# Early loads in one order with three groups in flight, and list writes at other steps, in an attention and expert-layer kernel

## The chip, the cores and the metric

The kernel runs on one core of a Trainium2 chip. The metric is device time in microseconds (us): three runs of the kernel before gave 456.02, 459.75 and 461.32 us, median 459.75. A core has TensorE (matrix products, written to PSUM), VectorE and ScalarE (elementwise work, both read PSUM), GpSimd (elementwise work on SBUF, and the DMAs whose rows come from an index list) and SyncE, which here only issues DMAs. Each engine works through its own queue in order; semaphores tell one of another. All DMAs run on the core's 16 DMA engines.

## The reference

Attention with a local window and a few global keys, and then a layer of experts in which each token goes to one expert. Shapes: B, H, S, D = 4, 8, 768, 64; 3072 tokens of 512 values, 8 experts, hidden width 1024, all in f32.

```python
scores = q @ k.T / sqrt(D) + bias            # bias: -slope(head) * distance, 96 local keys and 8 global ones
a = exp(scores - max); a = a / (a.sum() + 1e-9)
x = (a @ v)                                  # per token the 8 heads side by side: 3072 x 512
logits = x @ w_gate + modality_bias[modality_id]
e_idx = argmax(logits); gate_w = softmax(logits)[e_idx]
for e in range(8):                           # only the tokens of expert e
    out[mask] = gate_w * (relu(x[mask] @ w1[e]) @ w2[e])
```

## The kernel before

**Attention.** The tokens are 24 blocks of 128 (6 blocks for each of the 4 batches). The program goes in steps 0 to 24. Step n loads q and k of block n+2 and v of block n (`load_q`, `load_k`, `load_v`: one DMA for q, one for k, three for v, all on SyncE's queue), computes the scores of block n (`s_mm`, L228), the exponentials (`red`, L247 on VectorE and L258 on ScalarE), the transposes of block n-1's probabilities (`t_mm`, L272; their copies out of PSUM `t_cp`, L281 and L279) and the product with v of block n-2 (`pv`, L294 and L306; written "P·V" in the prediction), which `xr` scales and SyncE writes to the DRAM tensor `x_rows` (L334). q(n), k(n) and v(n) have three buffers each. Through `gate_a`, `gate_b` and `gate_c` the gate's logits of blocks n-3 and n-4 follow. Queue order of TensorE, VectorE and ScalarE is written out by hand in this part; SyncE's and GpSimd's order is made by the framework's scheduler, which simulates the program.

**What spaces the early loads.** `chained` (L120) counts groups of loads: two halves of q(0)/k(0) are groups 0 and 1, q(1) and k(1) group 2, then q(2)/k(2), v(0), q(3)/k(3), v(1), q(4)/k(4), v(2). A load in group j, with j from 3 to 8, waits until the last load of group j-2 has landed; later loads wait only for their buffers. The small constants (`consts_l`, L1070) are loaded in step 1's part of the program and wait for the latest group then opened, v(1).

**The lists.** When all six blocks of a batch have logits, its routing runs over the following steps (`route_a` to `route_f`; for the first three batches mostly on GpSimd, for the last on VectorE). It gives each token a row in a list sorted by expert, the DRAM tensor `ids_sorted`. `route_c` (L448) writes the list: six indirect DMAs on GpSimd for each batch, each of 128 rows. The first batch's are at steps 13 to 18, one each, the second's at steps 19 to 21, two each; each waits for the P·V product that was last in the program then (`by`, at first `pv_end`). The third's and fourth's are due after step 24, where `rest` takes up what is left over and calls one piece in each second place of the expert part: there the writes of the third batch wait for `last`, the latest activation of ScalarE in the program; those of the fourth for their data alone.

**Experts.** From the first two batches' lists (1536 tokens) `plan_parts` chooses three full tiles of 256 tokens of one expert, e0 to e2, so that the expert part can begin before the last two batches are listed. `ld_x` (L626) reads a tile's rows of the list on SyncE: at step 22, for all three. `gather_x` (L631) fetches the tokens from `x_rows` with two indirect DMAs on GpSimd, 128 rows of 2 KB each: at step 23 for e0 and 24 for e1; each waits for the step's P·V product. The weights of e0 (`rawe0a`, `rawe0b`) are loaded from step 19 on and split into a high and a low part (`split`) by ScalarE and VectorE.

After step 24 TensorE's queue has the transposes of e0 (`x_t`, L679, into PSUM buffers that block 23's probability transposes used just before), then P·V of block 23, the last gates, and the first layer (`l1_unit`, L696 to L698, three products per chunk). A tile then goes through 16 places m: m = 0 to 7 are the first layer, m = 8 to 15 the second (`l2`, L737 to L739). After each place `fill(u, m)` issues what comes next: pieces of `rest`, reads of lists, weights, gathers, splits. When the plan of all tokens is done (it needs the fourth batch's counts), `slist` holds 8 more full tiles s0 to s7 and 2 half ones, and `order` is extended by them; from then on s0's list is read, its weights loaded and its rows gathered. Beside s0 a slot of up to 32 tokens is computed (`few_...`), transposed at L759.

Of the kernel before, what the change touches and what calls it, by code (L numbers as in the profile page):

```python
# [28 lines left out]
NB = S // P  # L29
# [8 lines left out]
U = 256  # L38
NE = 3
NU = 8  # L40
NCHAIN = 9
BE = 2
NS = 8
NGR = 2
# [29 lines left out]
def moe_attention_kernel(  # L74
    ctx, tc, q, k, v, n_global, n_local, w1, q_t, k_t, v_l, v_s, small, w2, out
):
    nc = tc.nc
# [29 lines left out]
    last = [None]  # L107

    def spaced(ins, by=last):

        tc.add_manual_dep(
            ins.ins,
            by[0].ins.name,
            mybir.DependencyInfo(mybir.DependencyClass.Sync, mybir.DependencyReason.DATA),
            reason="spaced",
        )

    groups = []

    def chained(ins, ends=False):  # L120

        j = len(groups)
        if 2 < j < NCHAIN:
            spaced(ins, [groups[j - 2]])
        if j < NCHAIN and ends:
            groups.append(ins)

    def load_q(n):
# [274 lines left out]
    by = [pv_end]  # L403
# [207 lines left out]
    class Slot:  # L611
        straight = True

    fins, nraw = [], [0]

    def mk(name, e_src, o_src, inv_src, xsrc, halves):
        s = Slot()
# [4 lines left out]
    def ld_x(s):  # L622
        n = P * s.halves
        so = nc.sync.value_load(s.o_src, min_val=0, max_val=E * NT)
        s.ui = idp.tile([P, 2, 2], I32, tag="ui", name=f"ui{s.name}")
        nc.sync.dma_start(s.ui[:, 0 : s.halves, :], ids[ds(so, n), 0:2].rearrange("(t p) o -> p t o", p=P))  # L626
# [104 lines left out]
    def l2(s, fc, t):  # L731
        if fc == 0 and not s.po:
            s.po = {t: p_x(f"po{s.name}{t}") for t in range(2)}
        hi, lo = s.hi["b", fc // 2], s.lo["b", fc // 2]
        wv = slice(fc % 2 * 512, fc % 2 * 512 + 512)
        tt = slice(t * P, (t + 1) * P)
        nc.tensor.matmul(s.po[t], s.hh[:, fc, tt], hi[:, wv], start=(fc == 0), stop=False)  # L737
        nc.tensor.matmul(s.po[t], s.hh[:, fc, tt], lo[:, wv], start=False, stop=False)  # L738
        nc.tensor.matmul(s.po[t], s.hl[:, fc, tt], hi[:, wv], start=False, stop=(fc == 7))  # L739

    def few_in(s):
        so = nc.sync.value_load(s.o_src, min_val=0, max_val=E * NT)
# [269 lines left out]
    def at(n, f, *args):  # L1012
        todo.setdefault(n, []).append((f, args))
# [53 lines left out]
    mod = {}  # L1067

    def consts_l():
        spaced(nc.sync.dma_start(cst, small), [groups[-1]])  # L1070
        ints = cst[:, 144:196].bitcast(I32)
        mod["mb"] = cst[:, 128:144].rearrange("p (m e) -> p m e", m=2)
        mod["gi"] = ints[:, 0:4].rearrange("p (j w) -> p j w", j=2)
        mod["mi"] = ints[:, 4:52].rearrange("p (t w) -> p t w", w=2)
# [45 lines left out]
    LAST = NBLK - NB  # L1120
    for b in range(B):
        n0 = b * NB
        eng = nc.gpsimd if b + 1 < B else V
        at(n0 + NB + 3, route_a, b)
        at(n0 + NB + 4, route_e, b)
        at(n0 + NB + 4, route_b, b)
        at(n0 + NB + 5, route_d, b, eng)
        if b + 1 < B:
            at(n0 + NB + 6, route_f, b)
        for j in range(NB):  # L1130
            at(n0 + NB + 7 + (j // 2 if b else j), route_c, b, j)
    at(1, consts_a)
    at(3, consts_b)
    for j in range(8):
# [83 lines left out]
    at(LAST + 1, open_moe)  # L1218
    for c in range(4):
        at(LAST + 1 + c, lambda c=c: ld_w(eslots[0], "a", (c,)))  # L1220
    at(LAST + 4, lambda: [ld_x(s) for s in eslots])
    for u in range(GE):
        at(LAST + 5 + u, lambda u=u: gather_x(eslots[u], True))
    for n, c, h in ((2, 0, 0), (3, 0, 1), (4, 1, 0), (5, 1, 1), (5, 2, None), (6, 3, None)):
        at(LAST + n, split, None, "a", c, False, h)
    at(LAST + 6, lambda: ld_w(eslots[0], "b"))
# [102 lines left out]


    def rest():
        by[0] = last
        late = [job for n in sorted(todo) for job in todo[n]]
        writes = [args for f, args in late if f is route_c]
        g = planned([(f, args) for f, args in late if f is not route_c])
        while True:
            if writes and (writes[0][0], "pi") in rt:
                route_c(*writes.pop(0))
            try:
                next(g)  # L1340
            except StopIteration:
                break
            yield
        assert not writes

    def planned(late):
        for f, args in late:
            f(*args)
            if f is not route_e:
                yield  # L1350
        r = yield from items("b", plan, base[:, B - 1, NB, :], first_used, NI)
        uei, uoi, inv = slots("b", plan, *[t[:, 0:NS] for t in r], NS, 2)
        for u in range(NS):
            slist.append(mk(f"s{u}", uei[0:1, u : u + 1], uoi[0:1, u : u + 1], inv[:, :, u], xd, 2))
        fs.append(few_slot())
        yield
        gr = yield from granules(*r)
        uei, uoi, inv = slots("g", plan, *[t[:, 0:NGR] for t in gr], NGR, 1)
        for u in range(NGR):
            slist.append(mk(f"g{u}", uei[0:1, u : u + 1], uoi[0:1, u : u + 1], inv[:, :, u], xd, 1))  # L1360
        yield
        nl = NGT - NGR
        uei, uoi, inv = slots("l", plan, *[t[:, NGR:NGT] for t in gr], nl, 1)
        V.tensor_copy(lte[:, 0:nl], uei)
        V.tensor_copy(lto[:, 0:nl], uoi)
        V.tensor_copy(ltv[:, 0:nl], inv[:, 0, :])
        yield
# [4 lines left out]
    wrawb = sM.enter_context(tc.tile_pool(name="wrawb", bufs=RB, side="right", reuse_waits="tile"))  # L1372
    man = tc.manual_schedule(engines={ET.Activation})
    man.__enter__()
    bg = rest()
    fs = []

    nslot = NE + NS + NGR
    order = list(eslots)
# [2 lines left out]
    def fill(u, k):  # L1382

        s = order[u]
        nx = order[u + 1] if u + 1 < len(order) else None
        if u < NE and k % 2 == 0:
            next(bg, None)
        if len(order) == NE and len(slist) == NS + NGR:

            order.extend(slist[j] for j in ORDER)  # L1390
        if ahead[1] < min(len(order), u + 4):
            ld_x(order[ahead[1]])
            if ahead[1] == NE:
                few_in(fs[0])
            ahead[1] += 1
        if ahead[0] < min(len(order), u + 3):
            ld_w(order[ahead[0]])
            ahead[0] += 1
        if ahead[2] < min(len(order), u + 3) and ahead[2] < ahead[1]:
            gather_x(order[ahead[2]])  # L1400
            if ahead[2] == NE:
                few_x(fs[0])
            ahead[2] += 1
        if u == 0 and k in (4, 5, 6, 7):
            split(s, "b", k - 4)
        elif k < 8 and k % 2 and ("b", k // 2) in s.raw:
            split(s, "b", k // 2)
        if nx is None:
            return
        if s.halves == 1 and k == 3:  # L1410
            split(nx, "a", 0, early=True)
        if nx.halves == 1 and k in TB:
            split(nx, "b", TB.index(k))
        if s.halves == 1:
            if k in TG:
                split(nx, "a", TG.index(k) + 1)
        elif k >= 8 and k % 2 == 0:
            if ("a", k // 2 - 4) in nx.raw:
                split(nx, "a", k // 2 - 4)
        if s.halves == 2 and k in TX:  # L1420
            x_t(nx, TX.index(k))
# [157 lines left out]
```

## Time and profile before

| | |
|---|---|
| three runs | 456.02, 459.75, 461.32 us; median 459.75 |
| the profiled execution | 457.99 us, of which the span in the profile is 456.3 |
| mean granted TensorE clock | 0.985 |
| TensorE products busy | 437.4 us, 96% of the span |
| VectorE, ScalarE busy | 306.4 us (67%), 273.0 us (60%) |
| GpSimd busy | 117.9 us (26%) |
| DMA | 111.31 MB, mean 244 GB/s |

The profile shows one execution. Its times are counted from the start of the span. A row of a timeline has the start, the length, engine, source line, operation, out<-in by the program's names (numbers left out: `vx<-in_v_l` is the load of any block's v) and, in brackets, how long the engine stood idle just before and what released it. The releaser is inferred: where the engine named had long been done, it was another, often a DMA. SyncE only issues; its rows give the time of issue and not of landing. Busy shares of TensorE are modelled, since its products are pipelined. The granted clock is 1.00 at 2.4 GHz and 0.50 at 1.2 GHz.

### The profile page before, as it was taken

The page shows a single profiled execution, that of the slowest core. Times are in us where ns is not written, and L with a number is a line of the kernel's source. Part 1 is how long each engine was busy: PE and PEld are TensorE (multiplying, and loading weights), DVE is VectorE, ACT ScalarE, POOL GpSimd, SP SyncE. Part 2 cuts the span into 40 slices and gives each one's busy share as a digit, 9 for nine tenths or more (in the row PEclk, how much of TensorE's full clock was granted, in tenths as well). Part 3 has the DMA queues.
Part 4 walks back from the last instruction along what each step waited for, and adds up shares of the span by engine and source line. Part 5 has one row for each costly group of instructions (what it writes and reads, how often), then busy time and mean ns, then how long its engine had stood idle before and what let it go on. Part 6 is the DMA issues. An engine that isn't in the chain of part 4 may idle for free.

```text
span 456.3 us, 12951 instructions
## 1 busy us (share of the span) xinstructions
PE 437.4 (96%) x4856; PEld 382.9 (84%) x4856; DVE 306.4 (67%) x924; ACT 273.0 (60%) x674; POOL 117.9 (26%) x240
## 2 busy tenths in 40 slices
PE   7989999999899799999999999999999999999995
PEld 5778888888777698988889898898988989898993
DVE  7858888888697539688735659657496564647450
ACT  6858878878776336263635548645485554545541
POOL 8130011137726214805032211211312204010101
PEclk9989999999999799999999999999999999999998
DMA  7899999999998727557674767966679766655101
GB/s 249 277 306 328 356 351 362 353 332 328 301 303 283 270 68 246 204 190 268 224 245 146 251 212 256 368 212 226 229 237 368 263 214 237 206 203 186 47 2 52
DMA packets 41671, 111.31 MB, mean 244 GB/s; under 512 B 8815, under 2 KB 10863, under 8 KB 41600
## 3 DMA queue, kind: packets, MB, share of 16 engines
q1 hardware_dynamic: 36640, 97.07, 63.3%
q0 software_dynamic: 4672, 12.85, 7.6%
q8 instruction: 40, 0.66, 0.6%
q10 hardware_dynamic: 288, 0.48, 0.3%
q14 instruction: 31, 0.25, 0.2%
HBM read 96.01 MB, written 14.43 MB: 242 GB/s over the span
## 4 chain that ended last, share of the span: by engine, by line
PE 81%; issue 6%; DVE 4%; DMA 3%; POOL 3%; ACT 2%; SPq 0%; POOLq 0%; DVEq 0%
PE pt L272 7%; PE phs L696 6%; PE phs L698 6%; PE phs L697 6%; PE pos L739 6%; PE pos L738 6%; PE pos L737 6%; PE s L228 6%; PE x L306 5%; PE phe L698 3%; PE x L294 2%; PE phe L696 2%; PE phe L697 2%; PE tx L341 2%; PE poe L737 2%
## 5 line engine op out<-in xcount | busy, mean ns | idle before, releaser
L258 ACT ACTIVATE pr<-sc,nmx 128x168 f32<-128x168 f32 x192 | 81.1, 424 | 21.1 <-DVE nmx L247 21.1
L696 PE MATMUL phs<-xhs,ahs 128*128 128x256 f32 x256 | 72.4, 283 | 0.0
L698 PE MATMUL phs<-xhs,als 128*128 128x256 f32 x256 | 72.3, 283 | 0.0
L697 PE MATMUL phs<-xls,ahs 128*128 128x256 f32 x256 | 72.2, 282 | 0.0
L703 DVE SCALAR_TENSOR_TENSOR hls<-phs,hhs 128x512 fp32r<-128x512 f32 x32 | 22.1, 692 | 55.4 <-ACT hhs L702 55.4
L247 DVE CUSTOM_DVE_ANT_0 sc<-s,tbl 128x168 f32<-128x168 f32 x192 | 51.0, 328 | 8.7 <-PE s L228 7.8
L737 PE MATMUL pos<-bhs,hhs 128*128 128x512 f32 x128 | 51.4, 402 | 0.0
L631 POOL DMA_INDIRECT xgs<-x_rows,uis x16 | 19.9, 1246 | 121.9 <-DMA uis<-ids_sorted 55.7
L739 PE MATMUL pos<-bhs,hls 128*128 128x512 f32 x128 | 50.6, 395 | 0.0
L738 PE MATMUL pos<-bls,hhs 128*128 128x512 f32 x128 | 50.5, 395 | 0.0
L272 PE MATMUL pt<-ident,pr 128*128 128x128 f32 x288 | 45.3, 286 | 4.8 <-ACT pr L258 1.9
L696 PEld LDWEIGHTS phs<-xhs,ahs 128*128 128x128 f32 x256 | 49.0, 191 | 0.5 <-issue 0.2
L697 PEld LDWEIGHTS phs<-xls,ahs 128*128 128x128 f32 x256 | 48.9, 191 | 0.3
L698 PEld LDWEIGHTS phs<-xhs,als 128*128 128x128 f32 x256 | 48.9, 191 | 0.0
L702 ACT ACTIVATE hhs<-phs 128x512 fp32r<-128x512 f32 x32 | 19.1, 597 | 48.5 <-PE phs L698 42.7
L281 DVE COPY pT<-pt 128x384 f32<-128x384 f32 x73 | 38.2, 547 | 13.3 <-PE pt L272 12.6
L272 PEld LDWEIGHTS pt<-ident,pr 128*128 128x128 f32 x288 | 30.2, 141 | 17.1 <-DVE pT L281 5.7
L448 POOL DMA_INDIRECT ids_sorted<-tki,pi x24 | 25.8, 1074 | 49.8 <-issue 16.6
L228 PE MATMUL s<-kt,qt 64*64 64x168 f32 x768 | 36.7, 317 | 1.2 <-DVE nmx L247 1.0
L258 ACT ACTIVATION_READ_ACCUMULATOR pr<-sc,nmx 128x1 f32 x192 | 36.0, 188 | 0.0
L831 POOL DMA_INDIRECT out<-obs,ois x16 | 16.5, 1034 | 72.5 <-ACT obs L830 70.4
L228 PEld LDWEIGHTS s<-kt,qt 64*64 64x64 f32 x768 | 27.3, 136 | 4.7 <-ACT xT L343 1.3
(368 smaller groups left out, 1029.0 us busy)
## 6 DMA issues: line engine op xcount, KB each, us to landing
vx<-in_v_l SPq DMA_DIRECT2D x24, 512.0 KB
kt<-in_k_t SPq DMA_DIRECT2D x23, 464.0 KB
x_rows<-xr SPq DMA_DIRECT2D x24, 256.0 KB
qt<-in_q_t SPq DMA_DIRECT2D x23, 256.0 KB
vl<-in_v_s SPq DMA_DIRECT2D x48, 96.0 KB
rawe0a<-in_moe_w SPq DMA_DIRECT2D x4, 512.0 KB
rawe0b<-in_w SPq DMA_DIRECT2D x4, 512.0 KB
rawe1a<-in_moe_w SPq DMA_DIRECT2D x4, 512.0 KB
```

The lines of the kernel that those rows point to most:

```text
L228: nc.tensor.matmul(ps[h][64 * half : 64 * half + 64, c : c + W], qt[hs, hp, 64 * half : 64 * half + 64], kt[hs, hp, k0 : k0 + W], start=Tr ...
L247: V.tensor_tensor_reduce(out=sc, in0=pss[n, hp // 2][h][:, hp % 2 * W : (hp % 2 + 1) * W], in1=(tbl0 if n % NB == 0 else tbl)[:, hh, :], o ...
L258: last[0] = nc.scalar.activation(pr[:, h * (PRW - W) : h * (PRW - W) + W], sc, AF.Exp, bias=nmx[:, hh : hh + 1], scale=-1.0, accum_out=sum ...
L272: nc.tensor.transpose(tp[:, j * P : (j + 1) * P], pr[:, o : o + P], ident)
L281: V.tensor_copy(pT.rearrange("p a b -> p (a b)"), tp[:, 0 : 3 * P])
L448: ins = nc.gpsimd.indirect_dma_start(out=ids, out_offset=bass.IndirectOffsetOnAxis(ap=pi[:, j : j + 1], axis=0), in_=tki[:, b * NB + j, :] ...
L696: nc.tensor.matmul(o, hi[:, fs], s.xh[:, c, :], start=(c == 0), stop=False)
L697: nc.tensor.matmul(o, hi[:, fs], s.xl[:, c, :], start=False, stop=False)
L698: nc.tensor.matmul(o, lo[:, fs], s.xh[:, c, :], start=False, stop=(c == 3))
L737: nc.tensor.matmul(s.po[t], s.hh[:, fc, tt], hi[:, wv], start=(fc == 0), stop=False)
L738: nc.tensor.matmul(s.po[t], s.hh[:, fc, tt], lo[:, wv], start=False, stop=False)
L739: nc.tensor.matmul(s.po[t], s.hl[:, fc, tt], hi[:, wv], start=False, stop=(fc == 7))
```

## The change

It does four things.

- `chained`: a group of early loads waits for the group three ahead instead of two, and this holds up to group 10 (v(3)) instead of 8. Each load also comes behind the one before it in the queue, in the order in which the program calls them. The constants go through `chained` as well: they stand behind v(1) and ahead of q(4), and wait for v(0).
- The second batch's list writes are at steps 19 and 20, three each. The lists of e0 to e2 are read at step 21, e0's gather is at step 22, e1's at step 23.
- The twelve writes of the third and fourth batch are no longer called by `rest` but by `fill`, one after each place m = 8 to 15: eight beside e0's second layer, four beside e1's. The third batch's wait for `l2_end`, the latest product of the second layer in the program.
- `order` is extended by the remaining tiles only when all list writes have been called.

```diff
-NCHAIN = 9
+NCHAIN = 10
...
-    groups = []
+    groups, queue = [], []
 
     def chained(ins, ends=False):
 
         j = len(groups)
-        if 2 < j < NCHAIN:
-            spaced(ins, [groups[j - 2]])
-        if j < NCHAIN and ends:
+        if j > NCHAIN:
+            return
+        if j > 2:
+            spaced(ins, [groups[j - 3]])
+        if queue:
+            tc.add_manual_dep(
+                ins.ins,
+                queue[-1].ins.name,
+                mybir.DependencyInfo(mybir.DependencyClass.NoSync, mybir.DependencyReason.DATA),
+                reason="in order",
+            )
+        queue.append(ins)
+        if ends:
             groups.append(ins)
...
-        nc.tensor.matmul(s.po[t], s.hl[:, fc, tt], hi[:, wv], start=False, stop=(fc == 7))
+        l2_end[0] = nc.tensor.matmul(s.po[t], s.hl[:, fc, tt], hi[:, wv], start=False, stop=(fc == 7))
...
     def consts_l():
-        spaced(nc.sync.dma_start(cst, small), [groups[-1]])
+        chained(nc.sync.dma_start(cst, small))
...
         for j in range(NB):
-            at(n0 + NB + 7 + (j // 2 if b else j), route_c, b, j)
+            at(n0 + NB + 7 + (j // 3 if b else j), route_c, b, j)
...
-    at(LAST + 4, lambda: [ld_x(s) for s in eslots])
+    at(LAST + 3, lambda: [ld_x(s) for s in eslots])
     for u in range(GE):
-        at(LAST + 5 + u, lambda u=u: gather_x(eslots[u], True))
+        at(LAST + 4 + u, lambda u=u: gather_x(eslots[u], True))
...
     def rest():
-        by[0] = last
+        by[0] = l2_end
         late = [job for n in sorted(todo) for job in todo[n]]
-        writes = [args for f, args in late if f is route_c]
-        g = planned([(f, args) for f, args in late if f is not route_c])
-        while True:
-            if writes and (writes[0][0], "pi") in rt:
-                route_c(*writes.pop(0))
-            try:
-                next(g)
-            except StopIteration:
-                break
-            yield
-        assert not writes
-
-    def planned(late):
+        writes.extend(args for f, args in late if f is route_c)
         for f, args in late:
+            if f is route_c:
+                continue
             f(*args)
             if f is not route_e:
                 yield
...
         if u < NE and k % 2 == 0:
             next(bg, None)
-        if len(order) == NE and len(slist) == NS + NGR:
+        if k >= 8 and writes and (writes[0][0], "pi") in rt:
+            route_c(*writes.pop(0))
+        if len(order) == NE and len(slist) == NS + NGR and not writes:
 
             order.extend(slist[j] for j in ORDER)
```

Lines left out only declare `l2_end`, `writes` and `fs` earlier. LAST is 18, NB 6, NE 3.

## Rows read from the trace of the kernel before

**Rows 1.** The answer by stretches (us, each engine's busy time and count, TensorE's granted clock, DMA share, GB/s).

```profile
...
26.50:29.90 3.40, 3.40 (x68) 2.78 (x67) 0.00 (x0) 0.37 (x2) 1.54 (x8) 0.50 1.02 334
...
152.80:159.60 6.80, 6.33 (x70) 5.32 (x62) 2.94 (x7) 2.03 (x4) 1.78 (x2) 0.50 0.52 180
...
```

**Rows 2.** TensorE's timeline, steps 4 to 6 (start, length; in brackets idle before, releaser).

```profile
...
22.93 1.37 PE L228 MATMUL s<-kt,qt 64*64 64x168 f32 x32
26.10 1.38 PE L294 MATMUL x<-vl,pT 40*64 40x64 f32 x32 [1.79 <-DVE nmx L247]
...
32.17 1.57 PE L228 MATMUL s<-kt,qt 64*64 64x168 f32 x32
...
37.84 1.40 PE L228 MATMUL s<-kt,qt 64*64 64x168 f32 x32
...
```

**Rows 3.** SyncE's timeline (DMA issues), the early loads.

```profile
...
7.05 0.33 SPq L151 DMA_DIRECT2D vx<-in_v_l  x1
...
13.44 0.33 SPq L151 DMA_DIRECT2D vx<-in_v_l  x1
...
16.25 0.35 SPq L131 DMA_DIRECT2D qt<-in_q_t  x1
...
19.03 0.33 SPq L1070 DMA_DIRECT2D cst<-in_small  x1
19.40 0.43 SPq L151 DMA_DIRECT2D vx<-in_v_l  x1
...
```

**Rows 4.** TensorE's timeline, step 22 to the first layer.

```profile
...
132.02 1.15 PE L306 MATMUL x<-vx,pT 128*64 128x64 f32 x32
...
142.69 1.16 PE L294 MATMUL x<-vl,pT 40*64 40x64 f32 x32
...
149.98 0.63 PE L679 MATMUL mte<-ident,xge 128*128 128x128 f32 x4 [1.37 <-issue]
151.78 0.63 PE L679 MATMUL mte<-ident,xge 128*128 128x128 f32 x4 [1.18 <-DMA xge<-x_rows,uie]
152.34 0.82 PE L294 MATMUL x<-vl,pT 40*64 40x64 f32 x32
...
157.99 0.56 PE L696 MATMUL phe<-xhe,ahe 128*128 128x256 f32 x1
...
```

**Rows 5.** GpSimd's timeline, list writes and gathers.

```profile
...
122.34 0.97 POOL L448 DMA_INDIRECT ids_sorted<-tki,pi  x1 [0.30 <-issue]
...
128.67 0.97 POOL L448 DMA_INDIRECT ids_sorted<-tki,pi  x1 [0.30 <-issue]
...
143.48 1.10 POOL L631 DMA_INDIRECT xge<-x_rows,uie  x1 [1.10 <-DMA rawe0b<-in_w]
144.89 0.95 POOL L631 DMA_INDIRECT xge<-x_rows,uie  x1 [0.30 <-issue]
...
```

**Rows 6.** SyncE's timeline, steps 21 and 22.

```profile
...
129.48 0.35 SPq L151 DMA_DIRECT2D vx<-in_v_l  x1
...
135.15 2.15 SPq L626 DMA_DIRECT2D uie<-ids_sorted  x3
...
```

**Rows 7.** Stretches of 10 us, columns as in rows 1.

```profile
...
0.00:10.00 10.00, 7.56 (x96) 6.22 (x96) 6.74 (x46) 6.43 (x25) 8.65 (x49) 1.00 0.75 246
10.00:20.00 10.00, 8.50 (x187) 6.92 (x189) 9.32 (x51) 8.09 (x36) 2.68 (x5) 1.00 0.87 268
...
60.00:70.00 10.00, 9.97 (x235) 8.56 (x234) 8.79 (x51) 7.58 (x33) 2.83 (x15) 1.00 1.04 355
...
```

**Rows 8.** GpSimd's timeline, last list write and few-row gather.

```profile
...
189.75 0.97 POOL L448 DMA_INDIRECT ids_sorted<-tki,pi  x1 [0.30 <-issue]
...
211.02 1.03 POOL L749 DMA_INDIRECT xgf<-x_rows,uif  x1 [0.30 <-issue]
...
```

**Rows 9.** TensorE's timeline, second tile's second layer and few-row transposes.

```profile
...
197.48 0.39 PE L737 MATMUL poe<-bhe,hhe 128*128 128x512 f32 x1
...
221.51 0.43 PE L759 MATMUL mtf<-ident,xgf 32*128 32x32 f32 x4
...
```

More of the change, by code (lines that the diff above doesn't have):

```diff
@@ L612, in moe_attention_kernel @@
         straight = True
-    fins, nraw = [], [0]
+    fins, nraw, l2_end = [], [0], [None]
     def mk(name, e_src, o_src, inv_src, xsrc, halves):
@@ L1374, in moe_attention_kernel @@
     man.__enter__()
+    fs, writes = [], []
     bg = rest()
-    fs = []
     nslot = NE + NS + NGR
```

## The prediction

> **What bounds the kernel now.** I read the busy shares first (the table above): TensorE is at work in 96% of the span. So a change pays only where TensorE stands still or runs slowly. The windows and the granted clock show where: two stretches at 0.50, that is 1.2 instead of 2.4 GHz, 26.50 to 29.90 and 152.80 to 159.60 [rows 1]. Each follows a wait of TensorE, and I looked for the releaser of each in TensorE's timeline.
>
> The first: step 4's scores begin at 22.93; the P·V product of block 2 begins only at 26.10, after 1.79 us of idling, and the next step's scores at 32.17, while the next step takes 32.17 to 37.84 [rows 2]. The row names VectorE's nmx as releaser, but P·V does not read it; it reads v(2). SyncE issued vx(2) at 19.40, right behind the constants at 19.03, which wait for all of v(1); before that q(4) left at 16.25, when k(3) was there, and v(1) at 13.44, when v(0) was there [rows 3]. So v(2) was 6.7 us under way, and late because it was issued late.
>
> The second: TensorE ends the last attention step at 148.6 (149.98 less 1.37), idles 1.37 us, transposes one half of the first expert tile, idles 1.18 us, and gets to the first layer at 157.99 [rows 4]. The transposes read the gathered rows. GpSimd issued that gather at 143.48 and 144.89, though its row list was asked for at 135.15, itself 6.5 us after the last list write at 128.67 [rows 5, 6]; from 144.89 to 151.78 the second half took 6.9 us.
>
> **The change part by part, against the profiled execution** (457.99 us, 1.76 below the median 459.75 of the runs shown).
>
> *Early loads.* Before, a group waits for the one two ahead, constants for v(1); now for the one three ahead, in one order, and the constants stand before q(4). Then v(1) waits for k(2) and q(4), k(4) for v(0), which was there at 13.44; v(2) waits for k(3), there at 16.25 [rows 3], if nothing lands sooner. So v(2) leaves by about 16.3 instead of 19.40, and with 6.7 us it lands by 23.0, before the 24.3 (26.10 less 1.79) at which TensorE asks for it: an estimate with 1.3 us to spare. The DMA engines have room: their share is 0.75 in the first 10 us and 0.87 in the next [rows 7]. Step 4 took 9.24 us against 5.67 for the next [rows 2]: 3.57 us to win, the idle 1.79 and the half clock together. Bounds: 0, if v(2) stays as late; 3.6. I take 3.5. What is late next: k(5), q(5) and v(3), now waiting for groups of v(1) and k(4), needed at 28.4 and 29.8 instead of 32.2 and 33.5; they share the DMA time won. From 60 to 70 us the DMA share is 1.04 beside a full TensorE [rows 7]: little is to be had there, so the lead must come from the idle 2.5 + 1.3 us (0.25 and 0.13 of 10) of the first two windows, 3.8 us, which covers 3.5 barely.
>
> *Writes of the second batch's list in steps 19 and 20, list read in step 21, gathers in steps 22 and 23.* Step 20 issues its second write at 122.34 [rows 5]; the third, now the list's last, follows one write and its pause, 1.3, later: 123.7. With the old 6.5 us to the reads they leave at 130.2, and the three take 2.15 [rows 6]: 132.4. The gather then waits for step 22's P·V, which ends at 133.2 (132.02 plus 1.15, [rows 4]). Its second half leaves 1.4 later, at 134.6, and, with 6.9 us, is there at 141.5, 7 us before 148.6. So both waits go, 1.37 and 1.18, except some 0.4 for the PSUM copies that the transposes follow: P·V of the last block begins at 150.1 instead of 152.34 [rows 4], with no idle behind it that would lower the clock. From there to the first layer 5.65 us passed at 1.2 GHz; at 2.4 GHz I take 3.3, half and a little for waits between engines. The first layer starts at 153.4, 4.6 sooner, and its first 1.6 us at half clock (157.99 to 159.6) shrink by 0.7: 5.3. Bounds: 0 and 1.37 + 1.18 + half of 6.8, 5.95.
> Costs: two writes of 1.0 us each move from step 21 into steps 19 and 20, and one gather pair into step 22, all on GpSimd beside VectorE's copies. No row prices them; bounds −2 and +2 us from their own length, I take 0, since six writes stay six. The second tile's pair comes about where the first's stood. Behind the gather on GpSimd stands the routing of the third batch, up to 2.8 us later; its lists are needed only under the first expert tile. On SyncE the reads now stand before v(22) instead of behind it: see the rivals.
>
> *The last twelve writes.* Third-batch writes now wait for a second-layer product instead of an activation; fourth-batch writes wait for nothing new but are called later, and the remaining tiles are ordered only when none is left, one call later. TensorE waits for none of this: the last write left at 189.75 and the first gather from these lists that TensorE needs at 211.02, for a transpose at 221.51 [rows 8, 9]. With 6.9 us it is there at 217.9, 3.6 us early. Cost 0, covered by that spare; without it see the last rival.
>
> Sum: 457.99 − 3.5 − 5.3 = 449.2; the same off the median is 450.95. I put the prediction between, at **450.0**.
>
> **Rivals.**
> 1. *Only the move of the lists pays* (0.13). v(3) or k(5) is the next late load: the same wait comes one step on. For it: the DMA share above 1 in the loaded stretch. Against it: the idle share before. 457.99 − 5.3 = 452.7, 454.5 off the median.
> 2. *Only the start pays* (0.13). SyncE works in order; held until 130.2 by the list writes, then 2.15 us for the reads, it issues vx(22) not at 129.48 [rows 6] but near 134.0. With 6.7 us it lands at 140.7; TensorE wants it at 142.69 [rows 4], 2.0 later. If the writes land more than 2 us later than I take, TensorE waits in step 24, the clock falls there instead, and the second gain goes: 454.5, 456.3 off the median. The trace speaks a little against it by those 2.0 us.
> The Trainium skill's DMA: Bandwidth & Descriptors, Queues, rings and completion order, says that each DMA engine takes turns, packet by packet, between the queue rows that have work. By that rule the gather from GpSimd's queue would share the engines with v(22). Half a megabyte at the 355 GB/s of the full window [rows 7] is 1.5 us, which would leave 0.5 of the 2.0 us to spare: the sum stays 449.2, and this rival's 454.5 comes nearer. No row here shows the two together.
> 3. *It doesn't do what it says* (0.08): the scheduler leaves GpSimd's gather behind the routing, or SyncE's order as it was, and early loads come no sooner: 458 to 460.
> 4. *Slower* (0.06). With three groups in flight the early loads share the engines evenly instead of following each other, and each lands one group (3 us, 13.44 to 16.25) later. k(1), there at 7.05 when vx(0), which waits for it, leaves [rows 3], would come at about 10. TensorE would wait 3 us in steps 1 to 3, and of its 16 us of work in the first 20 (7.56 + 8.50, [rows 7]) some 7 would run at the lower clock and take twice as long: +10 − 5.3 on 457.99 is 462.7, 464.5 off the median. It decides once k(1) lands later than the bias tables, which GpSimd builds meanwhile, hide. Against it: before, each group was there in the order of issue, 2.8 to 3.4 us apart.
> 5. *Late last lists* (0.05). Emitted later, the fourth batch's last write may also run later: where it is called, behind the fourth product group (1.4 us each) of the second tile's second layer, which begins at 197.48 [rows 9]: 203.1 instead of 189.75. With 6.5 us to the reads, 2.15 for them, some 2 for their landing and 2.8 for the pair ahead, the few-row gather leaves at 216.6 instead of 211.02 and lands 2.0 past its transpose. With a half-clock stretch as after 152 (6.8 us, 3.4 lost) that is 5.4: 454.6. It costs nothing up to 3.6 us of delay.
>
> **Numbers.** The forecast, both gains within 1.5 us, has 0.55: 446.5 to 452.5. Rivals 1 and 2 add 452.7 to 456.3; the range **446 to 457** leaves out 3, 4 and the unknown. About 1% is what runs of this kernel can tell apart: faster means below 455.2. Faster 0.55 + 0.13 + 0.04 of rivals 2 and 5: 0.72. Same: the rest of 2 and 5 (0.14) and 3 (0.06): 0.20. Slower 0.08: rival 4 and a bad end of 3.
>
> **What would show it.** Start: no stretch at half clock near 26 us, step 4 to 5 about 5.6 us, vx(2) issued by 16.5. If vx(2) leaves early and TensorE still waits in step 5, rival 1. Lists: no wait over 0.5 us before the first transposes of the expert tile, no half clock there, gather near 133; if instead P·V of block 22 waits, rival 2. Last lists: a wait at the few-row transpose, rival 5. The step lengths from 30 to 110 us should stay at 5.5. The forecast is wrong if TensorE idles over 2 us anywhere between 20 and 155 us.

## The result, and the profile after

The changed kernel takes 456.08 us (median of 20 runs, 453.12 to 458.86) where the kernel before takes 459.74 (20 runs beside them): ratio 0.9919, 95% interval 0.9894 to 0.9945, so 3.7 us of gain where 8.8 to 9.7 were forecast. The profiled execution took 456.71 us, 1.3 under that of before; its last product starts at 448.83 instead of 450.19.

The page of the changed kernel: busy shares, the clock by slices, the queue of instructions.

```profile
PE 433.4 (95%) x4856; PEld 380.3 (84%) x4856; DVE 306.4 (67%) x924; ACT 273.9 (60%) x674; POOL 120.5 (26%) x240
...
PEclk9999999999999999999999999999999999999998
...
q8 instruction: 40, 0.66, 0.6%
```

The half clock is gone up to TensorE's last product, and still the span is hardly shorter. Line numbers are 10 higher than before. SyncE's issues, TensorE's scores of steps 4 to 6, and stretches, as [rows 3], [rows 2], [rows 1, 7]:

```profile
14.41 0.33 SPq L161 DMA_DIRECT2D vx<-in_v_l  x1
```

```profile
22.55 1.41 PE L238 MATMUL s<-kt,qt 64*64 64x168 f32 x31
...
28.20 1.60 PE L238 MATMUL s<-kt,qt 64*64 64x168 f32 x32
...
33.90 1.39 PE L238 MATMUL s<-kt,qt 64*64 64x168 f32 x32
```

```profile
26.50:29.90 3.40, 3.40 (x68) 2.91 (x70) 2.98 (x11) 2.32 (x9) 0.00 (x0) 1.00 1.03 291
50.00:60.00 10.00, 9.35 (x221) 8.30 (x221) 8.24 (x45) 6.94 (x28) 0.00 (x0) 1.00 1.04 347
60.00:70.00 10.00, 9.49 (x182) 8.13 (x181) 7.93 (x39) 8.30 (x35) 3.62 (x18) 1.00 1.03 338
...
80.00:90.00 10.00, 9.24 (x202) 7.97 (x200) 7.74 (x39) 7.27 (x29) 1.99 (x2) 1.00 1.03 344
...
152.80:159.60 6.80, 5.61 (x71) 4.74 (x66) 3.44 (x8) 2.56 (x5) 1.71 (x2) 1.00 0.80 267
```

vx(2) leaves at 14.41 instead of 19.40 and step 5 begins at 28.20 instead of 32.17: a lead of 3.97 us, and step 4 takes 5.65 us where it took 9.24. Then the lead is lost. P·V's second half (the products with vx) of block 3 starts 3.94 us sooner, of block 8 2.91, of block 11 1.46, of block 14 at 95.93 against 95.89 before. The stretch is full for the DMA engines (share 1.01 to 1.04), and TensorE is busy 9.2 to 9.5 of 10 us. Its timeline shows where it stands:

```profile
51.85 0.39 PE L304 MATMUL x<-vl,pT 40*64 40x64 f32 x10
52.67 0.57 PE L304 MATMUL x<-vl,pT 40*64 40x64 f32 x22 [0.42 <-issue]
...
58.71 0.50 PE L304 MATMUL x<-vl,pT 40*64 40x64 f32 x17 [0.23 <-issue]
...
65.14 0.46 PE L304 MATMUL x<-vl,pT 40*64 40x64 f32 x15 [0.51 <-issue]
...
71.70 0.44 PE L304 MATMUL x<-vl,pT 40*64 40x64 f32 x10 [0.74 <-issue]
...
83.97 0.27 PE L304 MATMUL x<-vl,pT 40*64 40x64 f32 x1 [0.73 <-issue]
...
90.56 1.04 PE L316 MATMUL x<-vx,pT 128*64 128x64 f32 x29 [0.59 <-issue]
```

Read the counts: 22, 17, 15, 10, 1 products of P·V's first half are left behind the stall, then 29 of the second half. The stall walks through the step. Counted from the head of the queue it comes at products 974, 1101, 1227, 1354, 1607 and 1733, that is at steps of 126 or 127 (with as many weight loads, some 253 instructions; the boundary near 1480 passes without a stall), while a step has 122. A late operand would stay at its place. Each stall ends 2.5 to 2.8 us after the start of one of the 40 packets of 16 KB on the instruction queue; at the seven boundaries that follow, none with a stall, the packet had begun 3.0 to 6.8 us before. I call them page stalls, a page being the instructions that one packet brings. Between starts of products the six cost 4.5 us (3.2 as idle time); the expectations below say 3.9, which is the sum without the one at 974.

The transition from the attention to the experts, as [rows 4], [rows 5] and [rows 6]: TensorE, then GpSimd, then SyncE.

```profile
143.66 1.13 PE L304 MATMUL x<-vl,pT 40*64 40x64 f32 x32
...
150.59 1.09 PE L689 MATMUL mte<-ident,xge 128*128 128x128 f32 x8 [0.50 <-ACT pT L289]
151.61 0.69 PE L304 MATMUL x<-vl,pT 40*64 40x64 f32 x32
...
155.52 0.39 PE L369 MATMUL lq<-sel,lps 128*128 128x8 f32 x2 [1.19 <-ACT lps L362]
155.76 0.36 PE L706 MATMUL phe<-xhe,ahe 128*128 128x256 f32 x1
```

```profile
124.36 0.96 POOL L458 DMA_INDIRECT ids_sorted<-tki,pi  x1 [0.30 <-issue]
...
134.41 1.10 POOL L641 DMA_INDIRECT xge<-x_rows,uie  x1 [5.59 <-DMA uie<-ids_sorted]
...
190.04 0.97 POOL L458 DMA_INDIRECT ids_sorted<-tki,pi  x1 [0.30 <-issue]
...
209.66 1.03 POOL L759 DMA_INDIRECT xgf<-x_rows,uif  x1 [0.30 <-issue]
```

```profile
130.72 2.19 SPq L636 DMA_DIRECT2D uie<-ids_sorted  x3
```

The gather leaves at 134.41 instead of 143.48, and of the two waits before the transposes 0.50 us is left, for the copies of block 23's transposes. Block 22's P·V is 0.97 us later than before, e0's first layer 2.2 us sooner. The gain is then lost once more, in e1's first layer: 181.51 to 196.52, 15.0 us against 13.0 before, with stalls for which the profile shows no releaser. The last list writes [rows 8], at 188.35 and 190.04, and the two writes of e0's results behind them in GpSimd's queue, at 191.32 and 192.62, run beside them:

```profile
191.97 0.28 PE L708 MATMUL phe<-xhe,ale 128*128 128x256 f32 x1 [0.59 <-issue]
...
193.42 0.38 PE L706 MATMUL phe<-xhe,ahe 128*128 128x256 f32 x1 [0.82 <-issue]
...
194.86 0.38 PE L708 MATMUL phe<-xhe,ale 128*128 128x256 f32 x1 [0.44 <-issue]
```

### The profile page after: what moved, and what is told of

It reads as the page before. It is cut to its first block, busy times and chain, and to the rows that moved or that the text cites. A ratio compares the mean times of both kernels' runs of the same rounds, so it can differ in the third digit from the quotient of the medians.

```text
span 455.0 us, 12952 instructions
## 1 busy us (share of the span) xinstructions
PE 433.4 (95%) x4856; PEld 380.3 (84%) x4856; DVE 306.4 (67%) x924; ACT 273.9 (60%) x674; POOL 120.5 (26%) x240
## 4 chain that ended last, share of the span: by engine, by line
PE 86%; issue 6%; POOL 3%; DVE 2%; ACT 2%; POOLq 0%; ACTq 0%
PE pt L282 8%; PE phs L706 6%; PE phs L708 6%; PE phs L707 6%; PE s L238 6%; PE pos L749 6%; PE pos L748 6%; PE pos L747 6%; PE x L316 5%; PE x L304 3%; PE phe L706 3%; PE phe L708 3%; PE phe L707 3%; PE poe L747 3%; PE poe L749 2%
## 5 line engine op out<-in xcount | busy, mean ns | idle before, releaser
L641 POOL DMA_INDIRECT xgs<-x_rows,uis x16 | 20.4, 1277 | 121.1 <-PE mts L689 73.7
L712 ACT ACTIVATE hhs<-phs 128x512 fp32r<-128x512 f32 x32 | 19.1, 598 | 48.4 <-PE phs L708 40.6
L458 POOL DMA_INDIRECT ids_sorted<-tki,pi x24 | 28.1, 1170 | 50.1 <-issue 20.4
L841 POOL DMA_INDIRECT out<-obs,ois x16 | 16.6, 1034 | 72.5 <-ACT obs L840 70.4
```

The lines of the kernel that those rows point to most:

```text
L458: ins = nc.gpsimd.indirect_dma_start(out=ids, out_offset=bass.IndirectOffsetOnAxis(ap=pi[:, j : j + 1], axis=0), in_=tki[:, b * NB + j, :] ...
```

## The experiments

Each set ran on one chip, with the kernel before timed beside it; the sets ran on five chips, here named by number; which chip the result above comes from is not on record. The ratios are those on record; the quotient of the medians shown differs from them by up to 0.0044. Theory A: the early lead is lost to TensorE's instructions coming late while the DMA engines are full. Theory B: v comes late. Theory C: the twelve writes' new places cost something.

### Chip 1: the parts alone, and less traffic

*Early loads alone* (the edits of `chained` and `consts_l`, `NCHAIN = 10`, on the kernel before).

> The kernel before with the new order and spacing of the early loads alone; lists, gathers and the last twelve writes stay as before. Theory A (late instruction pages): in the changed kernel the lead of 3.97 us at step 5 is spent between 50 and 96 us in stalls of TensorE of 0.45 to 0.96 us, each at one and the same count of instructions (every 253 or so) and 2.5 to 2.8 us after a 16 KB packet of the instruction queue began, while the DMA engines are full. It will be spent here too: the half clock near 26 us is gone, P.V of block 15 starts within 0.5 us of the kernel before, and the time is 0 to 0.7 us under it (ratio 0.9985 to 1.000). Rival (my forecast's step 1): the lead lasts to the end of the attention and the time is 3.0 to 3.8 us under (ratio 0.992 to 0.9935).

457.55 us, ratio 0.9953 (0.9928 to 0.9978). Between the two: some 2.1 us are gained, theory A's "0 to 0.7" is wrong as the rule, and so is my 3.5. In the profiled execution six page stalls (products 468, 595, 974, 1101, 1227, 1354; 2.9 us together) take the lead back: block 8 is level with before. That one execution says less than twelve timed ones.

*List moves alone.*

```diff
-            at(n0 + NB + 7 + (j // 2 if b else j), route_c, b, j)
+            at(n0 + NB + 7 + (j // 3 if b else j), route_c, b, j)
...
-    at(LAST + 4, lambda: [ld_x(s) for s in eslots])
+    at(LAST + 3, lambda: [ld_x(s) for s in eslots])
...
-        at(LAST + 5 + u, lambda u=u: gather_x(eslots[u], True))
+        at(LAST + 4 + u, lambda u=u: gather_x(eslots[u], True))
```

> The kernel before with the second batch's list writes at steps 19 and 20 and the reads and gathers one step earlier, nothing else. Theory A, by which the early loads bring nothing to the end: all of the changed kernel's gain is from here, the gather of e0 issues near 135 us, the first layer of e0 starts 2 to 4 us before that of the kernel before, and the time is 2.5 to 4 us under it (ratio 0.991 to 0.9945). Rival: the transition's gain is only the early loads' lead in other clothes; the time is within 1 us of before (ratio 0.998 to 1.002).

455.59 us, ratio 0.9934 (0.9909 to 0.9960): 3.0 us. From P·V's second half of block 22 to e0's first layer it takes 10.5 us; with the early loads alone 13.4. The rival is out. The start, whose loads are as before, came 2.3 us sooner than in the first profile of before (block 3), without a half clock near 26 us.

*Smaller zeroing*, on the changed kernel and on the kernel before.

```diff
-        idv = ids.rearrange("(p r) w -> p (r w)", p=P)
-        spaced(nc.sync.dma_start(idv[:, j * nid // 8 : (j + 1) * nid // 8], zrow))
+        r0 = j * NT + (0 if j == 5 else 1280)
+        idv = ids[r0 : r0 + 512].rearrange("(p r) w -> p (r w)", p=P)
+        spaced(nc.sync.dma_start(idv, zrow[:, 0:64]))
```

> The changed kernel, but of the list tensor only the 512 rows of each expert that lie round the end of its list are zeroed beforehand (the rows that are read past the lists' ends are among them): 8 writes of 32 KB instead of 8 of 194 KB, 1.29 MB less between 25 and 75 us, which is 3.7 us of DMA at the 345 GB/s of that stretch. Theory A: the stalls at the page boundaries fall from 3.9 us in sum to under 1.5, P.V of block 15 starts 2 to 3.5 us before that of the changed kernel, and half or more of this reaches the end: 1 to 3 us under the changed kernel (ratio to the kernel before 0.985 to 0.990). Theory B (the new order of loads makes v's data late, since the stalls sit in P.V): order and sizes of the loads are unchanged, so the stalls stay at 0.45 to 0.96 us each and the ratio at 0.992.

> The kernel before with the same smaller zeroing of the list tensor. Theory A: its TensorE comes 4 us later into the full stretch and stalls there for some 0.4 us in all, so there is next to nothing to win: P.V of block 15 within 0.6 us of the kernel before, ratio 0.998 to 1.000. Rival (the zero writes slow the attention in any case, by taking DMA time from the loads): 2 to 3.5 us gained as in the changed kernel, ratio 0.992 to 0.996.

On the changed kernel: 455.04 us, 0.9916 (0.9886 to 0.9945). After block 4 one page stall is left (0.37 us at product 974), before it there are two (0.74 and 0.39 at 468 and 595), with the same loads in the same order. That speaks against theory B, but weakly: on chip 2, below, the changed kernel has none in this stretch with the zeroing as it was. A lead of 2.1 us on the kernel before at block 4 is 2.4 at block 14:

```profile
70.00:80.00 10.00, 10.00 (x239) 8.87 (x231) 8.37 (x48) 8.27 (x37) 0.88 (x1) 1.00 1.00 332
```

But the time is that of the changed kernel. Block 22 is 2.4 us sooner than in the first profile of the changed kernel; 1.0 is left after the gates, since the granted clock is 0.50 from 154.5 to 157.9, and 0.7 at the end. Theory A's 1 to 3 us under the changed kernel did not come. On the kernel before: 457.83, 0.9973 (0.9945 to 1.0001), between the two expectations; not told apart.

### Chip 10: without the twelve, doubled writes, and the kernel before again

*Early loads and list moves, the last twelve writes as before* (both edits above), then *the same with the smaller zeroing*.

> The changed kernel without its last part: early loads and list moves as changed, the last twelve list writes called as in the kernel before. Theory C: the twelve writes' new places cost something. In the changed kernel the first layer of e1 takes 15.0 us with five stalls between 189 and 195 us, behind the fourth batch's writes; in the kernel before and with the lists moved alone it takes 13.0 us with three. Here it is 12.9 to 13.2 us, and the time is 1.2 to 2 us under the changed kernel (ratio to before 0.987 to 0.989). Rival (forecast's step 4: the twelve cost nothing): e1's first layer stays near 15 us, ratio 0.991 to 0.993.

> The same with the smaller zeroing of the list tensor (512 rows for each expert instead of all). If the two losses are separate (page boundary stalls by full DMA engines, e1's first layer by the twelve writes) they add: no stall over 0.3 us in P.V between 45 and 96 us, e1's first layer 13.0 us, ratio 0.984 to 0.988. If the transition at 145 to 160 us hides what the attention wins, it is no better than the kernel without the smaller zeroing (0.987 to 0.989).

448.39 us, 0.9861 (0.9821 to 0.9900), and 447.63, 0.9855 (0.9823 to 0.9887). Better than the changed kernel's 0.9919, but not for the reason expected: on this chip e1's first layer has no stalls in any kernel. From e1's first layer to e2's it is 23.55 us in the kernel before too, where chip 1 had 25.0 to 27.0. So this set does not test theory C, and ratios of different chips can't be set against each other. The smaller zeroing is again worth nothing at the end, and against the expectation it does not clear the page stalls: 0.94 us at product 595 and 0.62 at 1101 come even so.

*Each zero write twice.*

```diff
-        spaced(nc.sync.dma_start(idv[:, j * nid // 8 : (j + 1) * nid // 8], zrow))
+        for _ in range(2):
+            spaced(nc.sync.dma_start(idv[:, j * nid // 8 : (j + 1) * nid // 8], zrow))
```

> The changed kernel with each zero write of the list tensor made twice: 1.55 MB more between 25 and 75 us, 4.5 us of DMA at 345 GB/s. Theory A: the stalls of TensorE at its instruction pages grow from 3.9 us in sum to 6 to 9, P.V of block 15 starts 2 to 5 us later than in the changed kernel, ratio to before 0.996 to 1.004. If the stalls have to do with something else, P.V of block 15 moves by less than 1 us and the ratio stays at 0.992.

475.14 us, 1.0447 (1.0413 to 1.0481), far outside both. SyncE's queue says why:

```profile
46.00 6.77 SPq L1129 DMA_DIRECT2D ids_sorted<-zrow  x2
52.88 0.37 SPq L141 DMA_DIRECT2D qt<-in_q_t  x1
```

The second write goes to the rows of the first and waits until that has landed; the loads of q, k and v stand behind it, for some 6 us in each step. TensorE waits for k (15.5 us in eight waits), at half clock in between. My experiment measured a held queue, not traffic: the DMA share fell to 0.7.

*The kernel before, profiled again.*

> The kernel before, profiled a second time. The forecast took two half clock stretches of the first profile (26.5 to 29.9 and 152.8 to 159.6 us) as part of the kernel. Two other kernels with its early loads unchanged had no such stretch near 26 us and reached P.V of block 3 1.9 and 2.3 us earlier. If the stretches are chance of one execution, here at least one of them is gone or elsewhere, and P.V of block 3 starts 1.5 to 2.5 us before 33.5; if they belong to the kernel, both are there again within 2 us.

```profile
26.50:29.90 3.40, 3.40 (x58) 2.85 (x56) 1.79 (x6) 2.52 (x10) 1.01 (x5) 1.00 1.01 341
136.20:139.50 3.30, 3.30 (x20) 3.27 (x17) 1.97 (x5) 1.69 (x6) 0.00 (x0) 0.50 0.15 34
153.30:160.00 6.70, 5.07 (x79) 4.16 (x80) 2.17 (x5) 2.10 (x3) 1.89 (x2) 0.50 0.83 287
```

No half clock at 26.5, against [rows 1]; a new one at 136; the one at 153 is there. The second half of block 3's P·V starts 1.67 us sooner than in the first profile. And this kernel, with its old loads, falls 4.0 us behind the first profile between blocks 3 and 12, with five page stalls of 4.2 us (products 848, 974, 1101, 1354, 1607). So the stalls are not the change's alone; how many come differs from execution to execution.

### Chip 9: the parts beside each other

> The changed kernel itself, beside three of its parts on one chip, because the ratios measured so far come from different chips. Theory C (the twelve writes' new places cost): 0.4 to 0.6% over the kernel with the early loads and list moves alone. Rival (the chips differ): within 0.2% of it, whatever the level of both.

> Early loads and list moves, the last twelve writes as before. Theory C: 0.986 to 0.988 of the kernel before, and the changed kernel 0.991 to 0.993. Rival: both the same within 0.2%.

> The list moves alone. If the two parts add, this is 0.993 to 0.994 as measured, and 0.4 to 0.6% over the kernel with both parts. If the early loads' lead is spent in the full stretch (theory A), it equals the kernel with both parts within 0.2%.

> The early loads alone. If the parts add: 0.994 to 0.997 of the kernel before. Theory A: 0.9985 to 1.000.

| kernel | us | ratio to before (455.28) |
|---|---|---|
| changed | 449.11 | 0.9835 (0.9800 to 0.9869) |
| loads and lists | 449.75 | 0.9847 (0.9814 to 0.9880) |
| lists alone | 450.86 | 0.9901 (0.9869 to 0.9933) |
| loads alone | 453.59 | 0.9956 (0.9925 to 0.9987) |

The parts add (0.9901 x 0.9956 = 0.9857), and the twelve writes cost nothing here: 23.54 or 23.55 us from e1's first layer to e2's in all four. The whole change is worth 7.5 us on this chip by the ratio, 6.2 by the medians. Its transition with the loads alone, then with the whole change:

```profile
142.47 1.15 PE L316 MATMUL x<-vx,pT 128*64 128x64 f32 x32
...
148.16 0.63 PE L689 MATMUL mte<-ident,xge 128*128 128x128 f32 x4 [1.44 <-ACT ahe L678]
150.32 1.09 PE L689 MATMUL mte<-ident,xge 128*128 128x128 f32 x4 [1.54 <-DMA xge<-x_rows,uie]
...
155.73 0.37 PE L706 MATMUL phe<-xhe,ahe 128*128 128x256 f32 x1
```

```profile
144.37 1.15 PE L316 MATMUL x<-vx,pT 128*64 128x64 f32 x32
...
149.12 1.09 PE L689 MATMUL mte<-ident,xge 128*128 128x128 f32 x8 [0.50 <-ACT pT L289]
...
153.52 0.36 PE L706 MATMUL phe<-xhe,ahe 128*128 128x256 f32 x1
```

13.3 us against 9.2: the two waits for the gather are the difference, and what runs slower behind them.

### Chip 2: the twelve writes, more traffic, and moved pages

> The changed kernel again, beside the kernel without its last part. Theory C with its condition: where the kernels show stalls of TensorE in e1's first layer behind GpSimd's list writes (25.1 us from e1's first layer to e2's in the kernel before, 27.1 in the changed one), the twelve writes' new places cost 1.6 us, 0.3 to 0.4% over the kernel without them; where this stretch takes 23.5 us in all kernels, nothing.

> Early loads and list moves, the last twelve writes as before. Where TensorE stalls behind GpSimd's list writes: ratio to before 0.987 to 0.989 and 25.1 us from e1's first layer to e2's; where it does not: the same as the changed kernel, 0.983 to 0.987, and 23.5 us.

This chip has the stalls. Changed kernel 453.68 us, 0.9904 (0.9867 to 0.9941); without its last part 452.32, 0.9865 (0.9834 to 0.9896). The intervals overlap; the traces are the sharper test, since both executions run level to e1 (177.58 and 177.78):

```profile
177.58 0.28 PE L706 MATMUL phe<-xhe,ahe 128*128 128x256 f32 x1
...
187.87 0.28 PE L706 MATMUL phe<-xhe,ahe 128*128 128x256 f32 x1 [0.57 <-issue]
...
189.29 0.28 PE L707 MATMUL phe<-xle,ahe 128*128 128x256 f32 x1 [0.78 <-issue]
...
190.72 0.28 PE L708 MATMUL phe<-xhe,ale 128*128 128x256 f32 x1 [0.79 <-issue]
...
203.96 0.28 PE L706 MATMUL phe<-xhe,ahe 128*128 128x256 f32 x1
```

```profile
177.78 0.28 PE L706 MATMUL phe<-xhe,ahe 128*128 128x256 f32 x1
...
188.03 0.28 PE L707 MATMUL phe<-xle,ahe 128*128 128x256 f32 x1 [0.57 <-issue]
...
202.10 0.28 PE L706 MATMUL phe<-xhe,ahe 128*128 128x256 f32 x1
```

26.4 against 24.3 us: two stalls more, and the end is 1.86 us later. GpSimd's indirect DMAs end at 189.6 with the writes in their new places and at 187.2 in the old. Nor is it these two executions alone: of the ten profiles with such stalls, the five with the writes in their new places take 26.4 to 27.1 us here, the five with the old 24.3 to 25.2. Theory C holds, with its condition.

*One more zero write in each of steps 3 to 10, to a tensor that nothing reads*, and *58 warm-up products instead of 26*.

```diff
+        idv2 = spare.rearrange("(p r) w -> p (r w)", p=P)
+        nc.sync.dma_start(idv2[:, j * nid // 8 : (j + 1) * nid // 8], zrow)
...
-WARM = 26
+WARM = 58
```

> The changed kernel with one more zero write of 194 KB in each of steps 3 to 10, to a tensor that nothing reads, so that nothing waits for it (in the doubled writes the second waited for the first and held SyncE's queue for it). 1.55 MB more, 4.5 us of DMA at 345 GB/s, in the full stretch. Theory A (TensorE's instruction pages come late when the DMA engines are full): stalls over 0.4 us at the page boundaries (every 126 or 127 products: 848, 974, 1101, ...) between 25 and 96 us sum to 4 to 8 us against 0.9 to 4 in the changed kernel, P.V of block 15 is 1 to 4 us later, time 0.3 to 0.9% over the changed kernel. Rival: stalls and time as in the changed kernel within 0.2%.

> The changed kernel with 58 instead of 26 warm-up products, 64 more instructions at the head of TensorE's queue. Theory A: the stalls keep their counts from the start of the queue (product 974, 1101, 1227, 1354, 1480, ...), so that each now falls 32 products earlier in the step's work: before product 942, 1069, 1195, 1322 and 1448 of the changed kernel's count, in the scores instead of P.V, and the one at 2618 (first product of the gate's logits) before 2586. Rival (v or another operand is late): they stay at the same products of the program, 1006, 1133, 1259, 1386 here.

With the extra writes: 459.07 us, 0.9972 (0.9937 to 1.0008), 0.7% over the changed kernel beside it by the ratios. In these two executions the changed kernel has no page stall between 24 and 100 us, and with the extra writes there are five, at products 974, 1101, 1354, 1480 and 1607:

```profile
75.03 0.44 PE L305 MATMUL x<-vl,pT 40*64 40x64 f32 x10 [0.74 <-issue]
...
81.85 0.34 PE L305 MATMUL x<-vl,pT 40*64 40x64 f32 x6 [0.93 <-issue]
...
88.39 0.27 PE L305 MATMUL x<-vl,pT 40*64 40x64 f32 x1 [0.73 <-issue]
```

Block 14 is 7.8 us later, 3.9 of it from a later start with a half clock at 28.0 to 31.4, the rest in this stretch. With the longer warm-up alone no page stall came, so it told nothing of pages; but it told of e1's stalls: they came at products 3185 to 3203 of the program, where the other executions with the new places have theirs (3185 to 3208), with 32 more products ahead of them, and 17 to 22 us behind the last instruction packet. They are no page boundaries.

### Chip 3: traffic and moved pages together

> The changed kernel with the extra zero writes and with 58 warm-up products at once: the run with more warm-up products alone showed no stall in the full stretch, so it could not tell. Theory A: stalls over 0.4 us in the full stretch at some of the same counts from the start of the queue (848, 974, 1101, 1227, 1354, 1480, 1607, 1733), each 2.2 to 2.8 us behind the start of a 16 KB instruction packet. Rival (they belong to the step's work): at 1133, 1386, 1512 and 1639, 32 products later in the count, as with 26 warm-up products they were at 1101, 1354, 1480 and 1607.

454.98 us, one run. The stalls are at products 469, 721, 1733 and 2619 from the head of the queue and, of 0.3 us, at 1101 and 1227; 721 is 127 before 848, and 469 is 252 before that. At the rival's four counts there is none. At 1733 TensorE is now three products into P·V's first half; in the changed kernel it was three into the second half, 32 later in the program.

```profile
92.67 0.69 PE L305 MATMUL x<-vl,pT 40*64 40x64 f32 x29 [1.00 <-issue]
...
133.76 1.15 PE L317 MATMUL x<-vx,pT 128*64 128x64 f32 x31 [1.00 <-issue]
...
147.18 1.96 PE L317 MATMUL x<-vx,pT 128*64 128x64 f32 x32 [2.69 <-DMA vx<-in_v_l]
```

So the stalls keep to the queue: they come where TensorE passes from one instruction packet to the next, and this part of theory A is shown. That traffic sets their number is not. Counting those over 0.3 us between 24 and 100 us, the thirteen profiles with the zeroing as it was have 0 to 6, the three with less 2 or 3, the two with the extra writes 5 each; and in the 3 us before a boundary the DMA share is mostly 0.9 to 1.1 with a stall and without. The last row is the wait of my rival 2: v(22) late by 2.7 us. It came in one other profile, the lists alone on chip 9, with 0.53 us.

## Why the prediction was wrong

The order of events came nearly as worked out; the sizes did not. On chips where TensorE stalls, 3.5 us for the loads measured 2.1, 5.3 for the lists 3.0, and the last twelve writes, put at 0, cost 1.9.

**Early loads, −3.5 forecast; 0.9953 and 0.9956 measured, that is 2.1 and 2.0 us.** The mechanism was right in each point (vx(2) by 16.5, no half clock near 26, 5.65 us from step 4 to 5). The failed part is the size: "3.57 us to win, the idle 1.79 and the half clock together". The half clock at 26.5 was taken from one execution as a part of the kernel; of the five executions with the old loads that were profiled, the first alone had it. P·V's second half of block 3 starts at 34.13 in that one, at 31.26 to 32.47 (mean 31.95) in the other four and at 30.18 to 32.39 (mean 31.18) in eleven with the new loads and no added writes. So most of the lead of 3.94 us was that one execution's. Nor do the new loads rule a half clock out: it comes at 32.7 in the changed kernel on chip 9, behind a page stall of 1.93 us, and at 28.0 and 20.9 in the two profiles with extra writes.

**Lists, −5.3 forecast; 3.0 us (chip 1) and 4.5 us (chip 9, 0.9901) measured**, with intervals that overlap. List write, reads and gather came within 1.2 us of their forecast times (124.36, 130.72, 134.41 for 123.7, 130.2, 133.2). On chip 9 the transition went as worked out (P·V of the last block 150.15 for 150.1, first layer 153.52 for 153.4). Two terms failed. The half clock at 152.8 I charged in full, 6.8 us. It belongs to the old lists, but not always at this length: 6.8 us in both profiles of before, 3.4 in the two of the loads alone, none there with the smaller zeroing on the kernel before; with the lists moved a half clock came near there in two profiles (154.5 with the smaller zeroing, 147.2 behind the wait for v(22)). And for the moved writes "I take 0, since six writes stay six": where the chip stalls, the stretch from P·V's second half of block 17 to that of block 20 takes 19.0 to 19.4 us with the writes at the old steps (three profiles) and 19.1 to 20.4 at the new (seven, mean 19.9 against 19.2); on the other chips it is 16.6 to 18.1 with either. In the changed kernel's first profile TensorE also waited 1.19 us for the gate's copy, and P·V of the last block to the first layer took 4.15 us for the 3.3 that I took.

**The last twelve, "cost 0": wrong where the chip stalls.** I looked at who waits for the writes and priced none for what they do to TensorE beside them. 1.9 us at the end on chip 2; nothing on chip 9.

**"The step lengths from 30 to 110 us should stay at 5.5": wrong in the profiled execution** (6.0 to 6.6 in six of them). I had the warning, "the lead must come from the idle 2.5 + 1.3 us", but looked for late loads (rival 1) and not for late instructions. What the page stalls cost on the average stays open: the smaller zeroing left the time at the end as it was.

**Near by chance.** The 456.08 lies inside my range of 446 to 457, and inside rival 2's 454.5 to 456.3, but neither for its reason: the range covers late loads, and rival 2's wait for v(22) is in none of the changed kernel's three profiles. Rival 1's 452.7 to 454.5 is nearer than my 450.0 too; its reason, the next load late, is not what the trace shows.

**The sum.** Where TensorE stalls, the parts leave 2.1 + 3.0 − 1.9 = 3.2 of the 8.8 us, where 3.7 was measured. As ratios: 0.9953 x 0.9934 for loads and lists (chip 1), times 0.9904/0.9865 for the twelve (chip 2), gives 0.9926, and 0.9919 was measured for the change; with intervals of some 0.003 on each factor, so close a match is partly luck. Without stalls the change came to 0.9835 (0.9864 by the medians) for the 0.981 of my sum (449.2 of 457.99), still 1.3 to 2.6 us less. Why chips 1 and 2 stall behind GpSimd's writes and 3, 9 and 10 don't is not settled. The version to keep is loads and lists without the last part: 0.9861, 0.9847 and 0.9865 on three chips, as good as the changed kernel without stalls and, by the traces, better with them.

## What to carry to other kernels

Before a half clock stretch or a stall enters a sum, see it in a second profile of the same kernel: one of the two that I charged was of one execution alone. A lead of TensorE can be spent at its own instruction pages; find them by counting products from the head of the queue, since a stall that walks through a loop's body belongs to the queue and not to the data. Compare parts on one chip: the same change was worth 3.7 us on one and 6.2 to 7.5 on another.

## What the hardware showed that I had not expected

- TensorE's instructions come in packets of 16 KB over the same DMA engines, about 253 instructions of products and loads apart. Between 24 and 100 us a boundary with a stall cost 0.3 to 1.9 us between starts, and all but one of these stalls ended 2.2 to 2.9 us after a packet had begun. At product 2618, beside the loads of e0's weights, it cost up to 3.5 us, with a DMA share of 0.26 to 1.05 in the 3 us before, so full engines are not the whole of it. In all seven executions where that one was over 2 us the granted clock fell to 0.50 for 3.4 us about as it ended (at 136.2 in the second profile of before, the window shown above); in the three with 1.3 to 1.6 us it did not. The Trainium skill, Runtime: NRT & Kernel Launch, section Instruction fetch mechanics, says that instructions are refilled in blocks of 16 KiB (256 instructions) while the page before runs, and that crossing a boundary is "mostly hidden". The block agrees with the 40 packets of 16 KB; that it is hidden holds for most boundaries of these profiles, but not for the six above.
- TensorE stood still for 0.2 to 0.8 us at a time with GpSimd's indirect DMAs beside it and no semaphore to explain it; that these DMAs are the cause is argued from the moved writes alone: on chips 1 and 2 e1's first layer to e2's took 24.3 to 27.0 us (25.1 and 27.1 in the first two profiles), on chips 3, 9 and 10 it took 23.54 or 23.55 in every kernel.
- One DMA issue on SyncE that waits for the one before it to land held the queue for 6 us a step and put block 12's P·V 22 us behind the first profile of before.
